# Loads of w_out in quarters, the first tile's u on two queues, and another order in the first two quads

## The chip, the cores and the metric

The kernel runs on one core of a Trainium2 chip. The metric is the time of one execution on the device in microseconds (us); the value that counts is the median of several runs. The core has engines that each work through their own queue in order: PE (matrix products; its weight loads, PEld, overlap them), DVE (VectorE), ACT (ScalarE), POOL (GpSimd) and SP (SyncE, which only issues transfers). Transfers issued by SP or ACT run on 16 shared DMA engines. An engine that comes to an instruction whose input is not there waits, and everything behind it in its queue waits with it.

## The reference

Attention with normalised queries and keys, followed by a feed-forward block. Shapes: q, k, v (8, 12, 448, 64); w_in (768, 1024); w_out (1024, 768); everything is float32 except the three weights of the feed-forward block, which are float64.

```
q_n, k_n = q / sqrt(mean(q*q) + 1e-6) * g_q,  the same for k with g_k
attn = softmax(q_n @ k_n.T / 8);  x = attn @ v, as (3584, 768)
h  = x @ w_in                        # (3584, 1024)
u  = h * softmax(h)
ln = (u - mean(u)) / sqrt(var(u) + 1e-6) * g_ln
out = ln @ w_out                     # (3584, 768)
```

## The kernel before, in words

`fast_path` is what runs; `general_path` stands behind a test at the end and is not entered with these inputs. `fast_path` has two phases, and the order of every engine's work is written out by hand (`manual_schedule`): `unit(f)` runs one step of PE's work and then whatever had been put off with `later(n, f)` to the n-th unit from there. `follow` hangs such a piece of work on a part of the second phase.

**Attention.** 24 quads m of two pairs of heads (a = 2m, b = 2m + 1), so four heads a quad. For a pair, PE makes the scores of three blocks of keys (`scores`, L763), one block of the remaining keys for both pairs (`scores_last`, L776), the values (L796 and L807) and the sums of the exponentials (`sums`, L826). ACT takes the exponentials (L753) of each block; a score tile occupies one of three buffers of PSUM with tag "t" until then, and the tile of the sums, `sm`, comes from the same three. `inverse` (DVE L834, L835, then four small copies on POOL, L840) reads `sm` and so gives its buffer back; `divide` (L847, L848) writes the result `xo`, which `store_x` (SP, L853) puts into DRAM.

The next quads are prepared alongside. For a pair n: `load` (sixteen transfers per quad on SP, L602, each of 32 rows to 32 partitions), `squares` (ACT L624, one buffer), `row_sums` (DVE L632), `fold_sums` (POOL L642, L643), `rsqrt_seed` (ACT L662, L663), `rsqrt_step` (DVE L669 to L672), `normalise` (POOL L681), `qk_transpose` (DVE L691, which writes qkT) and `gain` (ACT L695, which scales the q half of qkT in place; `scores` and `scores_last` need it). The first two quads, m = 0 and m = 1, have an order of their own. `load_v` issues v (L615) and vl (L619) for the next quad.

**Weights.** w_in and w_out come as float64, viewed as pairs of 32-bit words, and are rounded to float32 on the chip, in 28 pieces: 12 of w_in (128 rows by 512 columns) and 16 of w_out (128 rows by 384 columns, 3072 bytes of each row). `load_w` issues the transfer of a piece (SP, L501); `convert_w` turns it into weights with two ACT instructions (L518, L519), two on DVE (L524, L525) and, for w_out, one more on ACT (L530). Twenty pieces are loaded and converted during attention, one a quad, from the fourth quad on (`load_next`, `begin`, `step`); of these the last eight are w_out's, loaded in the quads m = 13 to 20. There are two buffers for raw pieces. The last eight pieces of w_out are loaded together at the start of the second phase, into buffers that the attention's memory becomes, and are converted behind the first parts of the feed-forward block. POOL forms sums and differences of the weights (`combine`, L545).

Partition p = 32 g + j of w_out's piece c must hold row 256 g + 32 c + j, because DVE's transposition of u works in blocks of 32. Before the change one transfer reads all 128 rows through the view `(g c j) n -> c g j n`.

**Feed-forward.** 28 tiles t of 128 tokens in 14 groups g of two. Each product of two matrices is made with seven block products instead of eight (`products`, L918): per group seven with w_in (`in_parts`) and seven with w_out (`out_parts`, two groups later; LAG = 2). A product goes into one of five PSUM banks in turn, "tttoo"; the first is copied by ACT (L929), the others are added up by DVE (L925), and that frees the bank. When a tile's h is complete, its `ff_max` (DVE L972), `ff_exp` (ACT L978), `ff_mult` (DVE L982), `ff_moments` (DVE L990 to L995 and POOL L996), `ff_norm` (DVE L1000) and `ff_spread` follow, each one or more units later. Of each group the second tile comes first. `ff_spread` transposes u in blocks of 32 (DVE L1010) and moves the blocks to their places with sixteen transfers (L1016): a is the block of 32 tokens, g the group of 32 partitions. They are issued by SP, except for the tiles t = 0 and t = 26 (NT - 2), where ACT issues all sixteen. `block_sums` (POOL L898 to L902) makes the sums of blocks that the products need: `xsum` from x, `us` from u. x comes back from DRAM with `load_x` (L871; from the third group on issued by ACT). `load_again` and `check_w` (L554, L560, L561) read the weights once more for a check of their size.

Of the kernel before, what the change touches and what calls it, by code (L numbers as in the profile page):

```python
# [366 lines left out]
def fast_path(  # L367
# [24 lines left out]
    nc = tc.nc  # L392
    B, H, S, D = q.shape
    DM, DFF = moe_w_in.shape
    P = 128
# [5 lines left out]
    KF = DFF // P  # L401
    HO = DM // 2
    NT = B * S // P
# [81 lines left out]
    def load_w(step):  # L485
        src, c, i = step
        n = HO if src is moe_w_out else DFF // 2
        if second is None:
            raw = work.tile([P, DFF // 2, 2], U32, tag="raw", name="raw", bufs=2)[:, 0:n]
        else:  # L490

            tag, size, bufs = ("uT", KF * P, 2 * LAG + 2) if len(raws) % 2 else ("us", 3 * HF * P, 2)
            if tag == "us" and len(raws) >= len(wq) - 4:
                tag, size, bufs = "again", 2 * S, 2
            raw = second.tile([P, size // 2, 2], U32, tag=tag, name="raw", bufs=bufs)[:, 0:n]
        w = src.bitcast(U32)[:, 2 * i * n : 2 * (i + 1) * n]
        if src is moe_w_in:
            w = w[c * P : (c + 1) * P]
        else:
            w = w.rearrange("(g c j) n -> c g j n", g=4, j=32)[c]  # L500
        nc.sync.dma_start(raw.rearrange("p n t -> p (n t)"), w)  # L501
        return raw

    def convert_w(step, raw):
# [116 lines left out]
    def squares(n):  # L621
        d = st[n]
        d["sq"] = work.tile([P, 2 * NB, 32], FP32, tag="sq", name="sq", bufs=1)
        nc.scalar.activation(d["sq"], d["qk"].rearrange("p s b d -> p (s b) d"), AF.Square)  # L624
# [3 lines left out]
    def row_sums(n):  # L628
        m, i = divmod(n, 2)
        if i == 0:  # L630
            norms[m] = {"part": small.tile([P, 2, 2 * NB], FP32, tag="part", name="part", bufs=2)}
        nc.vector.tensor_reduce(norms[m]["part"][:, i], st[n]["sq"], AX, OP.add)  # L632
# [55 lines left out]
    def qk_transpose(n):  # L688
        d = st[n]
        d["qkT"] = work.tile([P, 2, S], FP32, tag="qkT", name="qkT", bufs=3)  # L690
        nc.vector.transpose(d["qkT"].rearrange("p s t -> p (s t)"), d["qkn"].rearrange("p b d -> p (b d)"))  # L691

    def gain(n):
        d = st[n]
        nc.scalar.activation(d["qkT"][:, 0], d["qkT"][:, 0], AF.Copy, scale=gcol[:, KF : KF + 1])  # L695
# [132 lines left out]
    def inverse(m):  # L828


        d = quads[m]
        r = work.tile([P, NB, 32], FP32, tag="r", name="r", bufs=1)
        rc = d["rc"] = small.tile([P, 2, NB], FP32, tag="rc", name="rc")
        nc.vector.transpose(r.rearrange("p b i -> p (b i)"), d["sm"])  # L834
        nc.vector.reciprocal(rc, r[:, :, 0].rearrange("p b -> p () b").to_broadcast([P, 2, NB]))  # L835
        for h in range(2):
            for i in range(2):
                a = 64 * h + 32 * i
                o = 64 * h + 32 * (1 - i)
                nc.gpsimd.tensor_copy(rc[o : o + 32, i], rc[a : a + 32, i])  # L840
# [166 lines left out]
    def ff_spread(t):  # L1007
        d = mt[t]
        ub = second.tile([P, DFF], FP32, tag="ub", name="ub", bufs=2)
        nc.vector.transpose(ub, d["u"])  # L1010
        uT = d["uT"] = second.tile([P, KF, P], FP32, tag="uT", name="uT", bufs=2 * LAG + 2)
        queue = nc.scalar if t in (0, NT - 2) else nc.sync
        for a in range(4):
            x = slice(a * 32, a * 32 + 32)
            for g in range(4):
                queue.dma_start(  # L1016
                    uT[g * 32 : g * 32 + 32, :, x], ub[x].rearrange("j (g c i) -> j g c i", g=4, i=32)[:, g]
                )
# [53 lines left out]
    def unit(f):  # L1072
        nonlocal now
        f()
        now += 1
        due = [x for x in todo if x[0] <= now]
        todo[:] = [x for x in todo if x[0] > now]
        for _, g in sorted(due, key=lambda x: x[0]):
            g()
# [34 lines left out]
    with tc.manual_schedule():  # L1114
# [19 lines left out]
        for m in range(NQ):  # L1134
            a, b = 2 * m, 2 * m + 1

            def outputs():
                values_last(m)
                values(a)


            next1 = m + 1 < NQ
            next2 = m + 2 < NQ
            next3 = m + 3 < NQ
            if m == 0:
# [12 lines left out]
                rsqrt_seed(norms["one", 2])  # L1158
                rsqrt_step(norms["one", 2])
                normalise(2)  # L1160
                add(a)
                unit(lambda: scores(b, 0))
                unit(lambda: scores(b, 1))
                unit(lambda: scores(b, 2))
                squares(3)
                row_sums(3)
                qk_transpose(2)
                fold_one(3)
                gain(2)
                rsqrt_seed(norms["one", 3])  # L1170
                add(b)
                rsqrt_step(norms["one", 3])
                normalise(3)
                load_v(1)
                load(6)
                load(7)
                for _ in range(2):
                    load_next()
                unit(outputs)
                squares(4)  # L1180
                row_sums(4)
                qk_transpose(3)
                unit(lambda: values(b))
                gain(3)
                squares(5)
                unit(lambda: sums(m))
                inverse(m)
                row_sums(5)
                fold_sums(2)
                later(1, lambda m=m: divide(m))  # L1190
                continue
            early = 1 < m and next1
            if early:
                rsqrt_seed(norms[m + 1])
                rsqrt_step(norms[m + 1])
                normalise(a + 2)
                normalise(b + 2)
            if next1:
                load_v(m + 1)
            unit(lambda: scores(a, 0))  # L1200
            store_x(m - 1)
            if early:
                qk_transpose(a + 2)
                if next3:
                    load(a + 6)
            unit(lambda: scores(a, 1))
            unit(lambda: scores(a, 2))
            unit(lambda: scores_last(m))
            add(a)
            unit(lambda: scores(b, 0))  # L1210
            if m == 1:
                rsqrt_seed(norms[m + 1])
                rsqrt_step(norms[m + 1])
                normalise(a + 2)
                normalise(b + 2)
                load(a + 6)
                load(b + 6)
            unit(lambda: scores(b, 1))
            if early:
                qk_transpose(b + 2)  # L1220
                if next3:
                    load(b + 6)
            if m >= NQ // 2:
                combine(w_in, m - NQ // 2)
            unit(lambda: scores(b, 2))
            if m == 1:
                qk_transpose(a + 2)
            if next2:
                squares(a + 4)
                row_sums(a + 4)  # L1230
            if next1:
                gain(a + 2)
            add(b)
            if m == 1:
                qk_transpose(b + 2)
            if next1:
                gain(b + 2)
            if next2:
                squares(b + 4)
                row_sums(b + 4)  # L1240
                fold_sums(m + 2)
            unit(outputs)
            step(m - 2)
            begin(m)
            step(m - 1)
            if m - 1 in sets:
                load_next()
            unit(lambda: values(b))
            if m == NQ - 1:
                block_sums(0, "A", 0)  # L1250
                block_sums(0, "A", 1)
                load_x(1)
            unit(lambda: sums(m))
# [13 lines left out]
        raw = {}  # L1267
# [92 lines left out]
```

## Time and profile before

| | |
|---|---|
| median of 3 runs | 908.34 us (908.28 to 909.74) |
| the profiled execution | 914.59 us |
| its span, first to last instruction | 912.8 us |
| granted PE clock, mean | 0.972 |
| busy: PE, DVE, POOL, ACT | 856.0, 649.6, 320.0, 315.3 us |

A line of the profile names the line of the kernel, the engine, the operation and the tiles, out<-in. In a timeline a line begins with the start and the duration in us, equal neighbours are put together (x8 is eight of them), and the bracket at the end is the idle time of the engine before it and what ended that. "PE L776" is a run on PE, "SPq" or "ACTq" an instruction of that engine's queue such as the issue of a transfer, "DMA raw<-in_moe_w_out_dram" in the chain of waits the time until that transfer had landed. In a table of waits the numbers are the total in us, how many times, and the longest. DMA share is the mean busy share of the 16 DMA engines.

### The profile page before, as it was taken

Reading aid. Unit: us, or ns where it says so; the run is one execution under the profiler, and the core shown is the slowest. Engines: PE = TensorE matmul, PEld = TensorE weight load, DVE = VectorE, ACT = ScalarE, POOL = GpSimd, SP = SyncE. Lnnn points to the kernel's source line nnn. Section 1 sums busy time; section 2 is a strip of 40 time slices with the busy share of each in tenths; the row PEclk is TensorE's granted clock in tenths of the full one; section 3 lists DMA queues with packets and bytes.
Section 4 is the critical chain, followed back from the end, with each engine's and each line's share of the span. In section 5 each row is a group of like instructions: output and inputs, shape, how many; then the busy total and the mean of one; then the engine's idle time right before and its main releaser. Section 6 shows DMA issues by size and latency. Waiting matters only on the chain.

```text
span 912.8 us, 12536 instructions
## 1 busy us (share of the span) xinstructions
PE 856.0 (94%) x4080; PEld 385.4 (42%) x4080; DVE 649.6 (71%) x1028; ACT 315.3 (35%) x475; POOL 320.0 (35%) x434
## 2 busy tenths in 40 slices
PE   5899999999988989968599999999999999999997
PEld 3233333333323323423255454554554554545554
DVE  5778988899868775457876685776866867756642
ACT  5577887787667664150201011011010110110100
POOL 1343444456434453505522421422314214212130
PEclk9999999999989989979799999999999999999999
DMA  6767787886656653232353544445444543331141
GB/s 124 177 148 151 190 191 148 187 192 125 149 128 124 159 133 92 80 114 50 87 148 88 128 115 111 112 85 140 119 90 107 141 101 77 74 64 52 29 110 44
DMA packets 350425, 106.92 MB, mean 117 GB/s; under 512 B 308880, under 2 KB 339600, under 8 KB 350352
## 3 DMA queue, kind: packets, MB, share of 16 engines
q1 hardware_dynamic: 327248, 94.93, 45.4%
q10 hardware_dynamic: 23104, 11.11, 4.6%
q8 instruction: 34, 0.56, 0.3%
q14 instruction: 39, 0.32, 0.1%
HBM read 69.28 MB, written 22.02 MB: 100 GB/s over the span
## 4 chain that ended last, share of the span: by engine, by line
PE 67%; DMA 11%; SPq 8%; DVE 6%; ACT 3%; issue 2%; POOL 2%; ACTq 1%; POOLq 0%; DVEq 0%
PE b L918 49%; PE s L763 6%; PE o L807 6%; DMA raw<-in_moe_w_out_dram 5%; SPq L602 5%; DMA v<-in_v_dram 4%; PE sm L826 3%; SPq L501 2%; ACT E L753 1%; PE s L776 1%; DVE es L786 1%; PE o L796 1%; DMA qk<-in_q_dram 1%; DVE part L632 1%; DMA raw<-in_moe_w_in_dram 1%
## 5 line engine op out<-in xcount | busy, mean ns | idle before, releaser
L918 PE MATMUL b<-w_in,xg 128*128 128x512 f32 x336 | 155.6, 607 | 9.1 <-ACT q L929 5.4
L918 PE MATMUL b<-w_out,uT 128*128 128x384 f32 x448 | 151.4, 486 | 0.0
L753 ACT ACTIVATE E<-s 128x896 f32<-128x896 f32 x168 | 140.2, 931 | 18.5 <-PE s L763 17.3
L763 PE MATMUL s<-qkT 64*64 64x448 f32 x1152 | 129.0, 577 | 3.7 <-DVE r L834 2.1
L918 PE MATMUL b<-w_in,xsum 128*128 128x512 f32 x252 | 119.3, 610 | 7.8 <-DVE h L925 5.3
L918 PE MATMUL b<-w_out,us 128*128 128x384 f32 x336 | 117.9, 495 | 6.1 <-POOL us L899 6.1
L807 PE MATMUL o<-E,v 128*64 128x448 f32 x576 | 113.5, 543 | 0.0
L996 POOL TENSOR_TENSOR he<-he,mhalf 128x1 f32<-128x1 f32 x28 | 17.2, 614 | 269.8 <-DVE he L995 269.8
L918 PEld LDWEIGHTS b<-w_out,uT 128*128 128x128 f32 x448 | 85.2, 190 | 62.0 <-issue 3.4
L918 PEld LDWEIGHTS b<-w_in,xg 128*128 128x128 f32 x336 | 65.1, 195 | 92.3 <-issue 75.1
L929 ACT COPY q<-b 128x512 f32<-128x512 f32 (+1 forms) x28 | 14.9, 530 | 255.2 <-PE b L918 239.7
L978 ACT ACTIVATE u<-h,hmax 128x1024 f32<-128x1024 f32 x28 | 32.2, 1149 | 194.9 <-DVE hmax L972 171.5
L681 POOL TENSOR_TENSOR qkn<-qk,ny 128x896 f32<-128x896 f32 x46 | 77.9, 1714 | 38.9 <-DVE ny L672 21.4
L918 PEld LDWEIGHTS b<-w_out,us 128*128 128x128 f32 x336 | 64.8, 193 | 52.0 <-POOL us L899 6.7
L763 PEld LDWEIGHTS s<-qkT 64*64 64x64 f32 x1152 | 48.4, 168 | 79.9 <-issue 37.8
L918 PEld LDWEIGHTS b<-w_in,xsum 128*128 128x128 f32 x252 | 48.8, 194 | 70.6 <-issue 59.9
L642 POOL COPY ss<-part 32x56 f32<-32x56 f32 x88 | 32.9, 373 | 117.2 <-DVE part L632 114.5
L807 PEld LDWEIGHTS o<-E,v 128*64 128x64 f32 x576 | 39.2, 137 | 72.6 <-issue 65.2
L786 DVE TENSOR_TENSOR es<-E 128x896 f32<-128x896 f32 x48 | 63.9, 1332 | 0.0
L925 DVE TENSOR_TENSOR h<-b,u 128x512 f32<-128x512 f32 x42 | 28.9, 687 | 41.8 <-PE b L918 41.8
L632 DVE TENSOR_REDUCE part<-sq 128x28 f32<-128x896 f32 x46 | 49.5, 1076 | 7.2 <-ACT sq L624 6.5
L925 DVE TENSOR_TENSOR u<-b,u 128x512 f32<-128x512 f32 (+1 forms) x56 | 34.6, 618 | 26.1 <-PE b L918 24.6
(103 smaller groups left out, 999.0 us busy)
## 6 DMA issues: line engine op xcount, KB each, us to landing
uT<-ub SPq DMA_DIRECT2D x416, 32.0 KB
xd<-xo SPq DMA_DIRECT2D x24, 448.0 KB
out_dram<-y SPq DMA_DIRECT2D x27, 384.0 KB
qk<-in_q_dram SPq DMA_DIRECT2D x184, 56.0 KB
qk<-in_k_dram SPq DMA_DIRECT2D x184, 56.0 KB
v<-in_v_dram SPq DMA_DIRECT2D x24, 384.0 KB
raw<-in_moe_w_in_dram SPq DMA_DIRECT2D x12, 512.0 KB
raw<-in_moe_w_out_dram SPq DMA_DIRECT2D x16, 384.0 KB
```

Source lines behind the costliest of these rows:

```text
L602: nc.sync.dma_start(d["qk"][g * 32 : g * 32 + 32, s], src[b, h0 + g // 2].rearrange("(b t) (x d) -> x t b d", t=32, x=2)[g % 2],)
L632: nc.vector.tensor_reduce(norms[m]["part"][:, i], st[n]["sq"], AX, OP.add)
L642: e.tensor_copy(ss[g * 32 : g * 32 + 32], part[o * 32 : o * 32 + 32])
L681: e.tensor_tensor(d["qkn"], d["qk"].rearrange("p s b d -> p (s b) d"), y.rearrange("p b -> p b ()").to_broadcast([P, 2 * NB, 32]), OP.mult,)
L753: nc.scalar.activation(d["E", kc], s[:, :, 0:S], AF.Exp)
L763: nc.tensor.matmul(s[c : c + D, h, 0:S], d["qkT"][hh, 1, keys], d["qkT"][hh, 0, :], start=True, stop=True,)
L786: nc.vector.tensor_tensor(d["es"], d["E", 0], d["E", 1], OP.add)
L807: nc.tensor.matmul(d["o"][h * D : (h + 1) * D, :], quads[n // 2]["v"][:, n % 2 * 2 + h, kc], d["E", kc][:, h], start=False, stop=(kc == NJ ...
L826: nc.tensor.matmul(sm[g : g + 32, :], w, e[:, h], start=(x == 0), stop=(x == len(terms) - 1))
L918: nc.tensor.matmul(o, a[:, c], w[:, i, c], start=(c == 0), stop=(c == last))
L925: nc.vector.tensor_tensor(out, k["o"], k[x], OP.add)
L978: nc.scalar.activation(d["u"], d["h"], AF.Exp, bias=d["nmax"], accum_out=d["s"])
```

## The change

In `load_w`, a piece of w_in is loaded as before, with one transfer. A piece of w_out is loaded with four transfers, one for each group g: 32 whole rows of the source to 32 partitions. In `ff_spread`, the tiles t = 0 and t = 26 have the eight transfers of the blocks a = 0 and 1 issued by SP and those of a = 2 and 3 by ACT. In the quad m = 0, the transposition of pair 3 goes behind `inverse`, and its `gain` moves into the quad m = 1, behind the second block of scores. In the quad m = 1, `gain` of pair b + 2 goes behind `squares` of pair b + 4.

```diff
-        if src is moe_w_in:
-            w = w[c * P : (c + 1) * P]
+            nc.sync.dma_start(to, w[c * P : (c + 1) * P])
         else:
-            w = w.rearrange("(g c j) n -> c g j n", g=4, j=32)[c]
-        nc.sync.dma_start(raw.rearrange("p n t -> p (n t)"), w)
+            for g in range(4):
+                r = (g * KF + c) * 32
+                nc.sync.dma_start(to[g * 32 : g * 32 + 32], w[r : r + 32])
...
-        queue = nc.scalar if t in (0, NT - 2) else nc.sync
         for a in range(4):
+            queue = nc.scalar if a > 1 and t in (0, NT - 2) else nc.sync
...
                 row_sums(4)
-                qk_transpose(3)
                 unit(lambda: values(b))
-                gain(3)
                 squares(5)
                 unit(lambda: sums(m))
                 inverse(m)
+                qk_transpose(3)
                 row_sums(5)
...
             unit(lambda: scores(a, 1))
+            if m == 1:
+                gain(b)
             unit(lambda: scores(a, 2))
...
-            if next1:
+            if next1 and m > 1:
                 gain(b + 2)
             if next2:
                 squares(b + 4)
+            if m == 1:
+                gain(b + 2)
+            if next2:
                 row_sums(b + 4)
```

More of the change, by code (lines that the diff above doesn't have):

```diff
@@ L496, in load_w @@
         w = src.bitcast(U32)[:, 2 * i * n : 2 * (i + 1) * n]
+        to = raw.rearrange("p n t -> p (n t)")
         if src is moe_w_in:
-            w = w[c * P : (c + 1) * P]
+            nc.sync.dma_start(to, w[c * P : (c + 1) * P])
         else:
-            w = w.rearrange("(g c j) n -> c g j n", g=4, j=32)[c]
-        nc.sync.dma_start(raw.rearrange("p n t -> p (n t)"), w)
+            for g in range(4):
+                r = (g * KF + c) * 32
+                nc.sync.dma_start(to[g * 32 : g * 32 + 32], w[r : r + 32])
         return raw
```

## The prediction

> **What bounds the kernel now.** I read the page first, then the busy times by stretch, then the PE timeline, and after that the queue of each engine at the places where PE waits. On the page, the shares of the chain that ended last, by line:
>
> ```profile
> PE 67%; DMA 11%; SPq 8%; DVE 6%; ACT 3%; issue 2%; POOL 2%; ACTq 1%; POOLq 0%; DVEq 0%
> PE b L918 49%; PE s L763 6%; PE o L807 6%; DMA raw<-in_moe_w_out_dram 5%; SPq L602 5%; DMA v<-in_v_dram 4%; PE sm L826 3%; SPq L501 2%; ACT E L753 1%; PE s L776 1%; DVE es L786 1%; PE o L796 1%; DMA qk<-in_q_dram 1%; DVE part L632 1%; DMA raw<-in_moe_w_in_dram 1%
> ```
>
> Two thirds are matmuls, which the change doesn't touch. The rest is w_out pieces (L501 and their landing), the q/k and v loads queued beside them, and small waits. The busy times by stretch say where (columns: stretch, its length, busy time and instructions of PE, PEld, DVE, ACT and POOL, granted clock, DMA share, GB/s):
>
> ```profile
> 0.00:52.00 52.00, 37.95 (x281) 15.12 (x281) 33.66 (x73) 29.29 (x46) 14.07 (x37) 0.97 0.70 144
> 52.00:211.00 159.00, 158.72 (x1340) 58.10 (x1333) 139.17 (x213) 125.41 (x180) 73.99 (x135) 1.00 0.77 173
> 211.00:354.00 143.00, 129.78 (x1016) 44.38 (x1016) 109.26 (x157) 94.30 (x137) 62.33 (x104) 0.94 0.59 133
> 354.00:455.00 101.00, 78.00 (x227) 31.76 (x220) 64.00 (x95) 25.29 (x43) 42.82 (x44) 0.89 0.30 86
> 455.00:912.80 457.80, 451.52 (x1241) 236.08 (x1240) 303.52 (x494) 41.04 (x73) 126.77 (x118) 0.99 0.40 97
> ```
>
> PE is full from 52 to 211 us and again from 455 on, so nothing is to be had there. It stands idle for 14 us before 52, 13 us in 211 to 354, and 23 us in 354 to 455, and in the last two the clock falls to 0.94 and 0.89. These are the stretches in which w_out comes in; w_in, larger by a third, came in during 52 to 211 and cost nothing. In the PE timeline each quad of heads has one run of L776:
>
> ```profile
> 64.17 0.93 PE L776 MATMUL s<-qkT 64*64 64x448 f32 x8
> ...
> 210.96 0.97 PE L776 MATMUL s<-qkT 64*64 64x448 f32 x8
> ...
> 353.91 0.93 PE L776 MATMUL s<-qkT 64*64 64x448 f32 x8
> ```
>
> Eleven quads took 146.79 us, 13.34 each; the next nine took 142.95, 15.88 each: 22.9 us more than nine at 13.34.
>
> **Part 1, the w_out pieces.** Who waits for them, in the table of waits; how long one takes to land, in the chain by time; and how busy the 16 DMA engines are while almost nothing but w_out is moving:
>
> ```profile
> ACT tmp L518 <- DMA raw<-in_moe_w_out_dram: 52.1, 16, 6.4
> ```
> ```profile
> 244.99 8.21 DMA raw<-in_moe_w_out_dram
> ```
> ```profile
> 376.00:403.00 27.00, 19.52 (x41) 7.92 (x39) 12.08 (x19) 9.01 (x16) 6.74 (x7) 0.91 0.26 103
> ```
>
> A share of 0.26 with eight transfers queued is 4 engines of 16 at full load: 384 KB run at 103 GB/s, some 3.8 us a piece, and whatever is queued behind them on these four engines waits too. The old source view begins with the 4 groups g, the new ones with 32 rows, like the q/k loads. So I read the change as: 4 engines before, 16 after. The Trainium skill ("DMA: Bandwidth & Descriptors", section "Why a DMA increments its semaphore by 16 and not by 1") says that such a DMA uses the largest number of engines up to 16 that divides the slowest dimension of both sides: 4 before, 16 after; the 0.26 agrees with the first half, and by this rule the sum is the one below.
>
> The attention quads. SP's queue:
>
> ```profile
> 206.35 1.98 SPq L602 DMA_DIRECT2D qk<-in_q_dram  x4
> 208.37 3.33 SPq L602 DMA_DIRECT2D qk<-in_k_dram  x4
> 211.81 0.61 SPq L501 DMA_DIRECT2D raw<-in_moe_w_out_dram  x1
> ...
> 215.02 5.32 SPq L602 DMA_DIRECT2D qk<-in_q_dram  x4
> ...
> 228.04 0.58 SPq L501 DMA_DIRECT2D raw<-in_moe_w_out_dram  x1
> ```
>
> Four q/k issues cost 1.98 us, or 0.50 each; right behind a w_out piece, v and xo they cost 5.32, since the four engines are still full. SP comes round in 16.23 us (211.81 to 228.04), later than PE needs it, so loads come late and ACT, whose queue is in order, holds back the exponentials behind L518. With 16 engines the jam goes, and the piece lands before ACT asks. What is late next is SP itself: w_out, v, vl and xd take 3.21 us (211.81 to 215.02), eight q/k issues 5.46 with one long one among them (206.35 to 211.81), the other eight about 4.1 (twice 1.98 and the gaps): 12.8. Three more issues at 0.50 make 14.3, against 13.34 for a quad, so SP falls behind by up to 0.96 in each of the eight quads that load a piece, 7.7 in all. Queued behind those issues are v, the xo store and the next q/k; they are asked for a quad ahead, which takes up some. Between 0 and 7.7 I take the middle, 3.7. Gain: 22.9 - 3.7 = 19.2 (15.2 to 22.9).
>
> The last eight pieces come when the attention's buffers are freed. SP, then DVE, whose converts L524/L525 stand between the additions that free PE's banks:
>
> ```profile
> 372.52 19.55 SPq L501 DMA_DIRECT2D raw<-in_moe_w_out_dram  x8
> 420.06 10.81 SPq L1016 DMA_DIRECT2D uT<-ub  x16
> ```
> ```profile
> 380.88 1.24 DVE L524 SCALAR_TENSOR_TENSOR tmp<-raw,tmp 128x384 uint32<-128x384 uint32 x1 [4.66 <-ACT tmp L519]
> ...
> 409.69 0.68 DVE L925 TENSOR_TENSOR u<-b,q 128x512 f32<-128x512 f32 x1
> ```
> ```profile
> 380.88:409.69 28.81, 20.60 (x38) 8.01 (x37) 16.59 (x24) 13.41 (x25) 2.02 (x2) 0.82 0.32 116
> ```
>
> From the first convert to the first addition after the last one DVE works 16.59 of 28.81 us; the rest it waits for pieces. Afterwards 32 issues at 0.50 take 16 us from 372.5, a piece about every 2 us instead of 3.8, the last landing near 391. The first convert moves up by 2.8 to 378.1 (of the 8.4 us from its piece's issue, 372.52, to 380.88, the 3.8 of transfer become 1.0); then DVE's own 16.6 us is the bound, plus some 1.9 for waits that remain among ACT, DVE and the pieces: 378.1 + 16.6 + 1.9 = 396.6 instead of 409.69. Gain 13.1 (9 if SP needs 0.6 an issue and DVE waits twice as long; 15 if DVE never waits).
>
> **Part 2, the first tile's u.** ACT's queue:
>
> ```profile
> 423.88 10.68 ACTq L1016 DMA_DIRECT2D uT<-ub  x16
> 434.61 1.15 ACT L978 ACTIVATE u<-h,hmax 128x1024 f32<-128x1024 f32 x1 [23.39 <-DMA uT<-ub]
> ```
>
> Sixteen issues hold ACT for 10.7 us, and the next tile's exponential, then DVE's product and PE's next copy, come after them. Eight issues fewer: 5.4 us earlier; the order behind is unchanged and DVE and POOL follow at once, so I count 5.4 (2 if DVE's other work fills in). The eight go to SP behind the other tile's sixteen (420.06 + 10.81 + 8 × 0.68 = 436.3); behind them wait the loads for the check, which nobody needs soon.
>
> The last tile but one is split as well. Tail of SP, POOL and PE:
>
> ```profile
> 871.69 10.68 SPq L1016 DMA_DIRECT2D uT<-ub  x16
> ```
> ```profile
> 883.85 1.26 POOL L898 TENSOR_TENSOR us<-uT 128x512 f32<-128x512 f32 x1 [12.86 <-DMA uT<-ub]
> ```
> ```profile
> 888.97 2.82 PE L918 MATMUL b<-w_out,uT 128*128 128x384 f32 x8
> ```
>
> Sixteen issues end at 882.4 and have landed by 883.85, 1.5 later. With eight more SP ends at 887.7 and they land at 889.2, 0.2 after PE wants this tile (888.97). I charge 0.2 (0 to 1).
>
> **Part 3, order in the first two quads.** DVE and PE:
>
> ```profile
> 30.20 1.11 DVE L691 STREAM_TRANSPOSE qkT<-qkn 128x896 f32<-128x896 f32 x1 [0.81 <-POOL qkn L681]
> 31.23 0.61 DVE L834 STREAM_TRANSPOSE r<-sm 128x448 f32<-128x448 f32 x1
> ...
> 46.53 1.09 DVE L632 TENSOR_REDUCE part<-sq 128x28 f32<-128x896 f32 x1 [1.58 <-ACT sq L624]
> ```
> ```profile
> 31.89 1.01 PE L763 MATMUL s<-qkT 64*64 64x448 f32 x8 [1.63 <-DVE r L834]
> ...
> 50.67 0.98 PE L776 MATMUL s<-qkT 64*64 64x448 f32 x8 [1.42 <-ACT E L753]
> ```
>
> The transpose of the fourth pair waits for POOL, and the inverse behind it frees the bank that PE wants. Put first, the inverse starts at 29.4 (30.20 less the 0.81 of waiting): 1.8 earlier. The scaling moved behind the first exponentials lets ACT start them earlier, but the pair's scores then wait for it; both fit into the same 1.8. In the second quad squares go ahead of the scaling that waits for DVE's transpose, so L632 loses its 1.58 wait. Only single DVE, ACT and four small POOL instructions move, no DMA. Gain 1.8 + 1.6 = 3.4 (1 to 4.5).
>
> **Sum.** 3.4 + 19.2 + 13.1 + 5.4 - 0.2 = 40.9. The profiled execution took 914.59 us (span 912.8), 6 us over the median of 908.34; none of the terms depends on that, so I take them from both: 873.7 there, and 867.4 for the median. Best ends: 4.5 + 22.9 + 15 + 5.4 = 47.8, 860.5. Weak ends: 1 + 15.2 + 9 + 2 - 1 = 26.2, 882.
>
> **The rivals.** *SP becomes the bound:* its 14.3 is taken up by nothing, and an issue costs 0.6 rather than 0.50. Quads 14.6 instead of 13.34: 8 × 1.26 = 10 lost instead of 3.7, and some 3 more in the last eight pieces: 877. For: SP has hardly a gap from 206 on. Against: loads are asked for a quad ahead. *DVE or ACT keeps the old pace after 372:* 5 of the 13.1 come: 875.5. For: DVE is busy 64 of 101 us there, and closing the gaps leaves it nearly full. *The pieces land no sooner* (memory, not four engines, sets 103 GB/s), but SP hides its issues: only parts 2 and 3 stay, 8.6: 900. Against: w_in's stretch moved 173 GB/s. *Slower:* the pieces land no sooner and each of 48 more issues lies on the path: 48 × 0.50 = 24 against 8.6 gained: 924. It decides once a split saves a piece's waiting by less than (24 - 8.6)/16 = 1.0 us; ACT's wait alone is now 52.1/16 = 3.3 a piece. The Trainium skill ("DMA: Bandwidth & Descriptors", section "Rules for kernel authors") speaks for this one: transfers to disjoint parts of the partitions serialize on the same engines, so one over 128 partitions should be used; no transfer quoted above tests it for 32 rows of 3 KB.
>
> **How the numbers follow.** Forecast 0.58 (861 to 872), SP bound 0.20, DVE or ACT 0.12, no sooner 0.04, slower 0.03, better than all ends 0.03. Range 860 to 882 leaves out the last three. Measurement of this kernel tells 0.2% (1.8 us) from no change. Faster by more: 0.96; within: 0.01; slower: 0.03.
>
> **What the profile after would show.** The DMA share well above 0.26 while the last eight pieces come, ACT's wait for raw near zero of 52.1, quads at 13.3 to 14.3 between the L776 runs, ACT's next exponential some 5 us after its first uT issue, and PE's wait for us L899 at 454 come some 37 us earlier. I am wrong if ACT still waits microseconds for raw, if the q/k issues behind a piece still take 5 us for four, or if DVE has gaps of several us between converts.

## The result, and the profile after

| | before | after |
|---|---|---|
| median | 909.04 us (908.28 to 912.4) | 870.77 us (870.16 to 872.16) |
| ratio, 95% interval | 1 | 0.9574 (0.9547 to 0.9602) |
| span of the profiled execution | 912.8 us | 868.3 us |
| granted PE clock, mean | 0.972 | 0.993 |

The change takes 38.3 us off the median; 40.9 were predicted. In the lines of after, numbers from the second half of the kernel are 2 to 4 higher: L501 is now L504, L518 L521, L602 L605, L776 L779, L899 L902, L918 L921, L925 L928, L978 L981, L1016 L1020; the kernels of the experiments have numbers of their own. On the page, the chain that ended last:

```profile
PE 77%; SPq 7%; DMA 4%; POOL 3%; issue 3%; DVE 3%; ACT 1%; ACTq 0%; POOLq 0%; DVEq 0%
PE b L921 51%; PE o L810 9%; PE s L766 9%; PE sm L829 5%; SPq L605 4%; DMA qk<-in_k_dram 2%; SPq L504 2%; PE s L779 2%; PE o L799 1%; DMA v<-in_v_dram 1%; ACT E L756 1%; POOL w_out L548 1%; SPq L1020 0%; DVE part L635 0%; POOL ss L645 0%
```

PE's share went from 67 to 77%, DMA's from 11 to 4%, and the landing of w_out pieces, 5% before, is no longer listed. The busy times by stretch, with the columns of before (the last stretch is shorter because the kernel ends sooner):

```profile
0.00:52.00 52.00, 40.92 (x311) 17.00 (x313) 36.90 (x77) 33.21 (x51) 16.45 (x38) 1.00 0.69 142
52.00:211.00 159.00, 158.56 (x1336) 57.67 (x1336) 138.64 (x213) 125.23 (x179) 74.74 (x134) 1.00 0.78 175
211.00:354.00 143.00, 142.17 (x1100) 51.52 (x1093) 119.62 (x170) 98.06 (x143) 74.08 (x119) 1.00 0.63 150
354.00:455.00 101.00, 89.69 (x221) 42.91 (x220) 84.56 (x126) 23.77 (x43) 41.46 (x39) 0.95 0.46 112
455.00:868.20 413.20, 406.94 (x1124) 212.76 (x1122) 273.65 (x446) 35.40 (x62) 114.27 (x106) 1.00 0.39 94
```

PE's idle time from 211 to 354 us went from 13.2 us to 0.8, and the clock there from 0.94 to 1.00. From 354 to 455 PE still stands idle for 11.3 of 101 us, with the clock at 0.95; of that more below. The waits for w_out pieces in ACT's queue (total, times, longest), and the PE timeline at the same three quads as before (and at the end of the longest of the last nine, which began at 274.63):

```profile
ACT tmp L521 <- DMA raw<-in_moe_w_out_dram: 4.2, 3, 2.8
```
```profile
60.29 0.56 PE L779 MATMUL s<-qkT 64*64 64x448 f32 x4
...
207.67 0.98 PE L779 MATMUL s<-qkT 64*64 64x448 f32 x8
...
289.02 0.98 PE L779 MATMUL s<-qkT 64*64 64x448 f32 x8 [0.83 <-ACT E L756]
...
329.16 0.93 PE L779 MATMUL s<-qkT 64*64 64x448 f32 x8
```

52.1 us of waiting became 4.2, the longest single wait 2.8. The nine quads with loads took 121.49 us (329.16 - 207.67), 13.50 each, where they had taken 142.95. SP's queue shows why, and that SP is still no faster than PE:

```profile
209.60 1.81 SPq L504 DMA_DIRECT2D raw<-in_moe_w_out_dram  x4
...
213.94 2.34 SPq L605 DMA_DIRECT2D qk<-in_q_dram  x4
...
222.64 2.77 SPq L504 DMA_DIRECT2D raw<-in_moe_w_out_dram  x4
...
236.60 2.22 SPq L504 DMA_DIRECT2D raw<-in_moe_w_out_dram  x4
...
307.31 1.80 SPq L504 DMA_DIRECT2D raw<-in_moe_w_out_dram  x4
```

The four issues of a piece take 1.81 us, 0.45 each. The four q/k issues that come after a piece, v and xo take 2.34 us where they took 5.32: SP no longer stands behind full engines. A round of SP takes 13.04 and then 13.96 us (from 209.60 to 222.64 and to 236.60), against 16.23 before. But over all seven rounds, from 209.60 to 307.31, it is 13.96 on average, longer than a quad of 13.34: SP falls 4.3 us behind PE. PE lost 1.4 us in the nine quads (121.49 against nine at 13.34), 1.05 of it in the one that ends at 289.02, 14.39 us long. In it ACT waits for a piece, and later PE for an exponential (0.83):

```profile
283.37 0.95 ACT L627 ACTIVATE sq<-qk 128x896 f32<-128x896 f32 x1 [1.56 <-DMA raw<-in_moe_w_out_dram]
```

The last eight pieces and what follows, in three stretches: from the last L779 to the first product with w_in, from there to the first addition after the last convert, and from there to the first product with us. First before, then after:

```profile
353.91:364.96 11.05, 11.05 (x92) 3.77 (x84) 5.83 (x7) 5.07 (x7) 6.78 (x5) 1.00 0.40 113
364.96:409.69 44.73, 36.52 (x78) 15.15 (x75) 23.06 (x33) 15.17 (x28) 12.68 (x16) 0.89 0.27 99
409.69:454.56 44.87, 30.08 (x62) 12.49 (x60) 34.79 (x55) 4.70 (x9) 23.01 (x23) 0.87 0.31 67
```
```profile
329.16:340.21 11.05, 11.05 (x92) 3.76 (x84) 5.83 (x7) 5.07 (x7) 6.78 (x5) 1.00 0.40 113
340.21:371.07 30.86, 30.86 (x76) 13.79 (x73) 24.33 (x34) 16.20 (x29) 13.75 (x16) 1.00 0.47 143
371.07:409.32 38.25, 26.94 (x64) 11.26 (x62) 34.70 (x55) 3.80 (x7) 23.02 (x23) 0.95 0.36 78
```

The second stretch is 13.87 us shorter, and PE is now busy through all of it at the full clock. While SP issues the last eight pieces in 32 transfers, the DMA share is 0.67, where it was 0.26:

```profile
348.14:362.86 14.72, 14.72 (x36) 6.56 (x35) 12.73 (x16) 8.99 (x17) 8.10 (x7) 1.00 0.67 199
```

The third stretch is 6.62 us shorter, and DVE is busy for 34.70 of its 38.25 us. In it, ACT's queue and then PE:

```profile
385.27 5.36 ACTq L1020 DMA_DIRECT2D uT<-ub  x8
390.67 1.15 ACT L981 ACTIVATE u<-h,hmax 128x1024 f32<-128x1024 f32 x1 [18.87 <-DMA uT<-ub]
```
```profile
399.37 2.82 PE L921 MATMUL b<-w_out,uT 128*128 128x384 f32 x8 [1.16 <-DMA uT<-ub]
409.32 2.93 PE L921 MATMUL b<-w_out,us 128*128 128x384 f32 x4 [7.13 <-POOL us L902]
...
844.55 2.85 PE L921 MATMUL b<-w_out,uT 128*128 128x384 f32 x8 [0.20 <-DMA uT<-ub]
```

Eight issues hold ACT for 5.36 us instead of 10.68, as predicted, and the exponential follows 5.40 us after the first of them. PE still waits 7.13 us for the sums of u at 409 us, the longest wait that is left. The first product with us begins 45.24 us sooner than before (454.56); the prediction's terms up to there add up to 41.1, and its list of signs has 37. At the end, the tile t = 26 lands 0.20 us too late: the 0.2 that was charged.

### The profile page after: what moved, and what is told of

The parts are those of the page before. It is cut to its first block, busy times and chain, and to the rows that moved or that the text cites. A ratio compares the mean times of both kernels' runs of the same rounds, so it can differ in the third digit from the quotient of the medians.

```text
span 868.3 us, 12637 instructions
## 1 busy us (share of the span) xinstructions
PE 838.3 (97%) x4080; PEld 381.9 (44%) x4080; DVE 653.4 (75%) x1028; ACT 315.7 (36%) x475; POOL 321.0 (37%) x434
## 4 chain that ended last, share of the span: by engine, by line
PE 77%; SPq 7%; DMA 4%; POOL 3%; issue 3%; DVE 3%; ACT 1%; ACTq 0%; POOLq 0%; DVEq 0%
PE b L921 51%; PE o L810 9%; PE s L766 9%; PE sm L829 5%; SPq L605 4%; DMA qk<-in_k_dram 2%; SPq L504 2%; PE s L779 2%; PE o L799 1%; DMA v<-in_v_dram 1%; ACT E L756 1%; POOL w_out L548 1%; SPq L1020 0%; DVE part L635 0%; POOL ss L645 0%
## 5 line engine op out<-in xcount | busy, mean ns | idle before, releaser
L921 PE MATMUL b<-w_out,uT 128*128 128x384 f32 x448 | 152.0, 488 | 1.4 <-DMA uT<-ub 1.4
L921 PE MATMUL b<-w_in,xg 128*128 128x512 f32 x336 | 151.3, 593 | 0.6 <-DVE h L928 0.6
L921 PE MATMUL b<-w_out,us 128*128 128x384 f32 x336 | 118.0, 495 | 7.1 <-POOL us L902 7.1
L766 PE MATMUL s<-qkT 64*64 64x448 f32 x1152 | 123.3, 555 | 1.1 <-DVE qkT L749 0.8
L921 PE MATMUL b<-w_in,xsum 128*128 128x512 f32 x252 | 115.1, 592 | 2.4 <-POOL xsum L902 2.4
L921 PEld LDWEIGHTS b<-w_out,uT 128*128 128x128 f32 x448 | 85.4, 191 | 64.1 <-issue 3.2
L981 ACT ACTIVATE u<-h,hmax 128x1024 f32<-128x1024 f32 x28 | 32.2, 1149 | 190.9 <-DVE hmax L975 172.0
L921 PEld LDWEIGHTS b<-w_in,xg 128*128 128x128 f32 x336 | 63.6, 190 | 79.4 <-issue 73.7
L921 PEld LDWEIGHTS b<-w_out,us 128*128 128x128 f32 x336 | 64.8, 193 | 53.0 <-POOL us L902 7.7
L921 PEld LDWEIGHTS b<-w_in,xsum 128*128 128x128 f32 x252 | 47.8, 190 | 63.1 <-issue 59.3
L928 DVE TENSOR_TENSOR h<-b,u 128x512 f32<-128x512 f32 x42 | 28.9, 688 | 41.8 <-PE b L921 41.8
L928 DVE TENSOR_TENSOR u<-b,u 128x512 f32<-128x512 f32 (+1 forms) x56 | 34.6, 619 | 26.1 <-PE b L921 24.5
```

The source lines that it names most:

```text
L766: nc.tensor.matmul(s[c : c + D, h, 0:S], d["qkT"][hh, 1, keys], d["qkT"][hh, 0, :], start=True, stop=True,)
L921: nc.tensor.matmul(o, a[:, c], w[:, i, c], start=(c == 0), stop=(c == last))
L928: nc.vector.tensor_tensor(out, k["o"], k[x], OP.add)
L981: nc.scalar.activation(d["u"], d["h"], AF.Exp, bias=d["nmax"], accum_out=d["s"])
```

## The experiments

My theory: the w_out pieces cost what they did because one transfer with an outer dimension of 4 kept to 4 of the 16 DMA engines; that is worth about 32 us, the first tile's u about 5, the order about 3. The rivals: that smaller transfers or more of them in flight help, whatever their shape; that SP's issues are the bound; and that what the order of the first quads gains doesn't reach the end.

**The parts alone.** Four kernels on one chip beside the kernel before (910.07 us).

Part 1 alone: the four transfers of 32 rows, and nothing else of the change.

```diff
...
-            w = w.rearrange("(g c j) n -> c g j n", g=4, j=32)[c]
-        nc.sync.dma_start(raw.rearrange("p n t -> p (n t)"), w)
+            for g in range(4):
+                r = (g * KF + c) * 32
+                nc.sync.dma_start(to[g * 32 : g * 32 + 32], w[r : r + 32])
```

> Only the four transfers per piece of w_out; the two queues for u and the order of the first quads as before. Theory A (the piece ran on 4 of 16 DMA engines, and that is what held up the quads and the last eight pieces): from the quad m = 14 to m = 23 the traces went from 142.95 to 121.49 us and the first convert to the addition after the last one moved 13.9 us, 35 in all; medians moved by 38.3, of which the other two parts should be 8 to 9, so this one is worth 30 to 35 us: 874 to 879 us. The first L776 of m = 2 stays at 50.7 us. Rival B (the parts are not independent: the jam in SP's queue also needs the earlier start of the first quads, or ACT's sixteen issues eat what the pieces give back): less than 24 us, above 884.

Measured: 876.87 us, ratio 0.9636 (0.962 to 0.9652). In the table of waits ACT's wait for raw is down, and in the PE timeline the nine quads take 120.15 us:

```profile
ACT tmp L521 <- DMA raw<-in_moe_w_out_dram: 5.5, 4, 2.8
```
```profile
210.61 0.97 PE L779 MATMUL s<-qkT 64*64 64x448 f32 x8
...
330.76 0.93 PE L779 MATMUL s<-qkT 64*64 64x448 f32 x8
```

By the ratio part 1 is worth 33.1 us (31.7 to 34.6) of 910.07, nearly the whole gain. The prediction had 32.3 for its two terms.

Part 2 alone: the u of the first tile and of the last but one on two queues.

```diff
-        queue = nc.scalar if t in (0, NT - 2) else nc.sync
         for a in range(4):
+            queue = nc.scalar if a > 1 and t in (0, NT - 2) else nc.sync
```

> Only the split of the first and the last but one u tile over SP and ACT. Theory A: ACT is free 5.3 us earlier, and all that follows (the exponential, DVE's product, PE's copy, us) moves with it: 5 us less, minus 0.2 to 0.7 at the end: 903.5 to 904.5 us, PE's wait for us ends 5.3 us earlier counted from the first convert. Rival B: us waits for POOL's own order or for u on SP, which now has 24 transfers to issue; then the exponential comes earlier but us does not: within 1.5 us of before.

Measured: 903.61 us, ratio 0.9937 (0.9917 to 0.9957), so 5.7 us (3.9 to 7.6).

Part 3 alone: the order of the first two quads.

```diff
-                qk_transpose(3)
                 unit(lambda: values(b))
-                gain(3)
...
                 inverse(m)
+                qk_transpose(3)
...
             unit(lambda: scores(a, 1))
+            if m == 1:
+                gain(b)
...
-            if next1:
+            if next1 and m > 1:
                 gain(b + 2)
             if next2:
                 squares(b + 4)
+            if m == 1:
+                gain(b + 2)
+            if next2:
                 row_sums(b + 4)
```

> Only the order of inverse, transposition and scaling in the first two quads. Theory A: the 3.9 us by which the L776 of m = 2 comes earlier (50.67 to 46.79) stay to the end: 904.5 us. Rival B: in the quads that load w_out the pace is set by SP and the transfers, not by PE, so an earlier start is waited away there: L776 of m = 2 at 46.8 as well, but the L776 of m = 23 less than 1.5 us earlier, and the time above 907.

Measured: 908.69 us, ratio 0.9989 (0.9973 to 1.0006): 1.0 us (-0.5 to 2.5), not to be told from nothing. The PE timeline of this kernel at the third and the fourth quad:

```profile
46.84 0.98 PE L776 MATMUL s<-qkT 64*64 64x448 f32 x8 [0.67 <-ACT E L753]
...
62.10 0.61 PE L776 MATMUL s<-qkT 64*64 64x448 f32 x4 [0.84 <-ACT E L753]
```

The third quad begins at 46.84 instead of 50.67, 3.8 us sooner. One quad on, 62.10 against 64.17, it is 2.1: PE waits 0.84 us more for an exponential there, and the rest of the loss isn't assigned. The rival was nearer in the time, but its mechanism is not what the trace shows: the run of the last quad begins at 344.49, 5.75 us sooner than in the trace of the unchanged kernel below, where it should have come less than 1.5 sooner. This profiled execution, 904.03 us, was the fastest of twelve; what the typical one loses, and where, stays open.

The kernel before once more, unchanged, to see how much two executions of one kernel differ.

> The kernel before, unchanged, profiled once more: its profiled execution took 914.59 us and its median is 908.3 to 909.0, while the traces of before and after differ by 44.5 us and the medians by 38.3. Theory A: the 6 us are waits that vary from one execution to the next, in the quads that load w_out (142.95 us from m = 14 to m = 23 in the first trace): a profile of 908 to 910 us has 137 us there and the same stretches elsewhere. Rival B: profiling adds them everywhere: again 914 to 915 us, with 143 there.

Measured: 909.64 us, ratio 1.0002. Its profiled span is 907.8 us, 5.0 less than that of the first profile, and the PE timeline shows most of that in one place:

```profile
210.79 0.96 PE L776 MATMUL s<-qkT 64*64 64x448 f32 x8
...
350.24 0.93 PE L776 MATMUL s<-qkT 64*64 64x448 f32 x8
```

The nine quads took 139.45 us here, 142.95 in the first profile, and 136.61 and 135.36 in those of parts 2 and 3, which have the old loads too. So what the slow loads cost is not a fixed number: 3.5 us apart in two executions of one kernel, 7.6 over these four traces of three kernels. In seven traces with the quarters, these nine quads took 120.15 to 122.89 us.

**What about the four transfers helps.** First one transfer, but of 128 consecutive rows:

```diff
-        if src is moe_w_in:
-            nc.sync.dma_start(to, w[c * P : (c + 1) * P])
-        else:
-
-            for g in range(4):
-                r = (g * KF + c) * 32
-                nc.sync.dma_start(to[g * 32 : g * 32 + 32], w[r : r + 32])
+        nc.sync.dma_start(to, w[c * P : (c + 1) * P])
```

> The changed kernel with each piece of w_out loaded by one transfer of 128 consecutive rows, as w_in's pieces are, in place of four transfers of 32 rows; the product with w_out then uses rows of w_out in another order, so this run is only for its time. Theory A (what the four transfers gain is the spread over all 16 DMA engines): one transfer whose outer dimension is 128 rows does the same with a quarter of the issues. ScalarE's wait for raw pieces stays at a few us, the nine quads with loads take 120 to 121.5 us as with the quarters, the queue's issues no longer come near its bound, and the kernel takes 866 to 871 us. Rival B (it is the size or the number of the transfers that counts, a single large one being slow whatever its shape): the waits for raw are back and the kernel takes 895 to 910 us.

Measured: 869.72 us, ratio 0.9552 (0.9526 to 0.9578), the same as the change. SP's queue has 8 issues in place of 32 for the last eight pieces. In the busy times, the DMA share while they land is 0.97, and from the first convert to the first addition after the last PE has no gap:

```profile
348.93 3.70 SPq L498 DMA_DIRECT2D raw<-in_moe_w_out_dram  x8
```
```profile
350.00:357.50 7.50, 7.50 (x19) 3.37 (x18) 6.81 (x8) 5.04 (x9) 5.30 (x5) 1.00 0.97 342
353.26:371.88 18.62, 18.62 (x44) 8.18 (x44) 18.34 (x25) 14.50 (x26) 6.95 (x6) 1.00 0.45 152
```

So neither the number nor the size of the transfers made the gain: one large one does it if its outer dimension is long. A quarter of the issues brings nothing further that can be told from noise. SP's round falls to 13.28 us with it (seven rounds from 210.18 to 303.16), PE's pace, but the nine quads take 120.75 us, no less than the 120.80 that they take on average in seven traces with quarters: the few us by which SP falls behind with four don't show. Then the other way, two transfers of 64 rows:

```diff
-            for g in range(4):
-                r = (g * KF + c) * 32
-                nc.sync.dma_start(to[g * 32 : g * 32 + 32], w[r : r + 32])
+            v4 = w.rearrange("(g c j) n -> c g j n", g=4, j=32)[c]
+            for h in range(2):
+                nc.sync.dma_start(to[h * 64 : h * 64 + 64], v4[2 * h : 2 * h + 2])
```

> The changed kernel with each piece in two transfers of 64 rows, each with an outer dimension of 2 and runs of 32 rows behind it. Theory A (the number of engines of a transfer follows its outer dimension): each transfer uses 2 engines, a piece needs about twice the time that it needed as one transfer of outer dimension 4, the DMA share in the stretch of the last eight pieces is about 0.13, eight pieces take about 60 us there, and the kernel is slower than before the change: 940 to 980 us. Rival B (smaller transfers, more of them in flight, are what helps): between the 870 of the change and the 908 of before, about 885 us.

Measured: 961.23 us, ratio 1.057 (1.0538 to 1.0602): 52 us slower than before, with transfers half as large and two in place of one. The table of waits, SP's queue and the busy times while the last eight pieces come and nothing else is moving:

```profile
ACT tmp L520 <- DMA raw<-in_moe_w_out_dram: 106.8, 16, 10.1
```
```profile
392.64 48.91 SPq L503 DMA_DIRECT2D raw<-in_moe_w_out_dram  x16
```
```profile
410.00:449.00 39.00, 11.56 (x17) 4.38 (x18) 9.11 (x15) 7.81 (x14) 0.00 (x0) 0.65 0.13 52
```

ACT's wait doubled, and an issue took SP 3.06 us (48.91/16) against 0.46 in the change; I read that as SP waiting for room, which no view shows by itself. 52 GB/s and a share of 0.13, two engines' worth, stand against 103 and 0.26 with one transfer of outer dimension 4: half, as expected. This kills the rival of smaller transfers. It also speaks against slower engines or a slower memory as the cause: among the trace's DMA packets, those of 3072 bytes, the rows of w_out, took 0.123 us each in the kernel before and 0.124 here, but before, four of them were in flight at a time (23.8 of the 27 us from 376 to 403), and here two (42.4 of the 45 us from 410 to 455). So transfers that wait behind one another used no more engines than one alone. The Trainium skill ("DMA: Bandwidth & Descriptors", section "Why a DMA increments its semaphore by 16 and not by 1") has the number of engines follow the slowest dimension: for 128, 32, 4 and 2 the order of the times agrees, its 4 agrees with the share of 0.26 before, and its 2 with the 0.13 here.

Eight transfers of 16 rows:

```diff
             for g in range(4):
-                r = (g * KF + c) * 32
-                nc.sync.dma_start(to[g * 32 : g * 32 + 32], w[r : r + 32])
+                for h in range(2):
+                    r = (g * KF + c) * 32 + h * 16
+                    p = g * 32 + h * 16
+                    nc.sync.dma_start(to[p : p + 16], w[r : r + 16])
```

> The changed kernel with each piece in eight transfers of 16 rows: the same bytes over the same engines with 32 more issues in every eight pieces. Theory A (SyncE's issue of transfers is near its bound already with four per piece): at 0.45 us for an issue a quad grows by 1.8 us of issue, of which 1.3 to 1.8 shows, 10 to 16 us over nine quads; the last eight pieces are 64 issues, 29 us against 14.7, which adds 8 to 14 us; 888 to 900 us in all. Rival B (the issues lie beside other work and have room): less than 875 us.

Measured: 898.54 us, ratio 0.9878 (0.9848 to 0.9908). SP's queue in the quads and at the last eight pieces:

```profile
225.25 3.65 SPq L505 DMA_DIRECT2D raw<-in_moe_w_out_dram  x8
...
240.39 4.55 SPq L505 DMA_DIRECT2D raw<-in_moe_w_out_dram  x8
...
320.56 4.64 SPq L505 DMA_DIRECT2D raw<-in_moe_w_out_dram  x8
```
```profile
363.15 30.59 SPq L505 DMA_DIRECT2D raw<-in_moe_w_out_dram  x64
```

A round of SP takes 15.14 us from 225.25 to 240.39 and 15.89 on average over the six rounds to 320.56. PE's nine quads take 135.25 us: the first three still 13.26 to 13.50 us each, the other six 15.05 to 16.37. From the fourth on SP sets the pace. The 64 issues at 0.48 us take 30.59 us, and the stretch from the first product with w_in to the addition after the last convert is 45.10 us, 14.2 longer than with four transfers. With four transfers SP is the slower engine too, by 0.6 us a round; over eight pieces that doesn't reach PE, presumably because the loads are asked for a quad ahead. With eight it is slower by 2.5, and that shows.

**What is left at 409 us.** PE's 7.13 us wait there is for `us` on POOL. In the trace after, POOL makes the four sums over x first (402.27 to 406.66 us), though the sums over u are wanted sooner. Three things put otherwise:

```diff
-            queue = nc.scalar if a > 1 and t in (0, NT - 2) else nc.sync
+            queue = nc.scalar if t == NT - 2 or (t == 0 and a > 1) or (t == 1 and a == 3) else nc.sync
...
-            follow(p, 2 if g > LAG else 4, lambda: block_sums(g - LAG, "U", 0))
+            follow(p, 2 if g > LAG else 1, lambda: block_sums(g - LAG, "U", 0))
```

> The changed kernel with three things put otherwise: the transfers of the second-last tile's u all on ScalarE's queue as before the change; one more transfer of the second tile's u on ScalarE's queue; and the sums over the first u blocks follow one part earlier, so that they stand ahead of the other sums on GpSimd. Theory A (TensorE's 7.13 us wait for the sums of u, and the late second-last tile, are the loss that is left of the change): the wait shrinks to 1 to 3 us and 0.2 us come back at the end: 864 to 868 us. Rival B (VectorE, dense from 371 to 414 us, is the bound of that stretch, and whatever GpSimd does earlier only moves the wait): 869.5 to 872 us.

Measured: 867.27 us, ratio 0.9526 (0.9498 to 0.9554), 4.4 us below the change by the two ratios, whose intervals touch. In the PE timeline the wait fell from 7.13 to 0.78 us, and a new one came:

```profile
404.08 2.82 PE L921 MATMUL b<-w_out,us 128*128 128x384 f32 x8 [0.78 <-POOL he L999]
...
433.85 2.93 PE L921 MATMUL b<-w_in,xsum 128*128 128x512 f32 x3 [2.58 <-DVE y L928]
```

Behind it, in the timelines of SP and DVE, stands the second reading of the weights:

```profile
407.71 19.91 SPq L1020 DMA_DIRECT2D uT<-ub  x28
427.71 1.02 SPq L557 DMA_DIRECT2D again<-in_moe_w_in_dram  x2
```
```profile
432.19 0.62 DVE L563 TENSOR_REDUCE extent<-again 128x1 f32<-128x448 f32 x1 [6.31 <-DMA again<-in_moe_w_in_dram]
```

The transfer is issued only at 427.71, behind 28 issues of u, and DVE, which takes its work in order, stands 6.31 us before the reduction that needs it; the addition that PE wants is behind that. The last four kernels were run beside each other on one chip. The change itself:

> The changed kernel itself, beside the three others on one chip, so that they can be compared with it and not only with the kernel before. 869 to 872 us.

Measured: 871.82 us, ratio 0.9592 (0.9571 to 0.9613). The change without part 3, that is with the diff of part 3 taken back (its removed lines stand again, its added ones don't):

> The changed kernel with the order of the first quads put back to that of before; the quarters and the first tile's u on two queues stay. Theory A (the 3.9 us that the order gains before the third quad are partly taken back in that quad: 1.8 us are left at its end in five of the six traces that have the order): 871 to 873 us, 1 to 2 above the changed kernel of this call. Rival B (the whole gain stays, as in the changed kernel's own trace): 873.5 to 875 us. Rival C (nothing stays): the same as the changed kernel within 0.5 us.

Measured: 871.52 us, ratio 0.9577 (0.9556 to 0.9598), 0.3 below the change: rival C, nothing stays. The profiled executions of the two differ by 2.5 us the other way (spans 869.8 and 867.3), so a single profile of each would have said that the order gains.

The kernel with the three things put otherwise, the early sums over u among them, and in addition the second reading fourteen parts of PE's work later (the products of one group; its third transfer is issued at 454.07 us instead of 425.72):

```diff
-            follow(parts, (2 * LAG + 1 + 2 * (x // 3)) * 7 - 7 * LAG + (0, 4, 5)[x % 3], lambda x=x: check_next(x))
+            follow(parts, (2 * LAG + 1 + 2 * (x // 3)) * 7 + (0, 4, 5)[x % 3], lambda x=x: check_next(x))
```

> The changed kernel with the second-last tile's u all on ScalarE's queue again, a fourth part of the second tile's u on ScalarE's queue, the first sums over u ahead of the other sums on GpSimd, and the second reading of the weights for their extent two groups later, so that it doesn't stand in SyncE's queue behind the first tiles' u. Theory A (without the late reading the 6.5 us gained before the product with us are kept: the 2.58 us wait of TensorE at 434 us and the half clock behind it are gone): 863 to 866 us. Rival B (another wait of the same size takes its place on VectorE or SyncE, or the end of the kernel now waits for the check): 867 us or more.

Measured: 862.55 us (861.93 to 863.62), ratio 0.9482 (0.9462 to 0.9502): 9.3 us below the change on the same chip, somewhat better than the theory's best. The 2.58 us wait is gone. The busy times of 405.3 to 415.5 us, in the change and here, show that the 7.13 us wait had cost more than itself:

```profile
405.30:415.50 10.20, 6.18 (x10) 3.46 (x11) 9.08 (x12) 2.85 (x5) 6.35 (x6) 0.50 0.57 125
```
```profile
405.30:415.50 10.20, 9.29 (x29) 5.23 (x30) 10.13 (x12) 2.85 (x5) 6.54 (x6) 1.00 0.39 91
```

In the change the granted clock falls to 0.50 during the wait, at 405.3 us, and stays there until 415.5, 6.2 us after PE has work again. How long it stays isn't fixed: in the second trace of the change, behind a wait of 7.15 us, it is back at 412.0, 2.8 us after PE has work. In the kernel with the late reading, where the wait is 0.74 us, it is 1.00 throughout, and PE gets 29 products done in these 10.2 us instead of 10.

The same without part 3:

> The kernel with the early sums over u and the late second reading, and with the order of the first quads put back to that of before. Theory A (the order is worth 1 to 2 us): that much above the kernel with it in this call. Rival B (worth nothing): within 0.5 us of it.

Measured: 863.66 us (863.29 to 864.67), ratio 0.9498 (0.9477 to 0.9518), 1.1 above the kernel with it: theory A at its low end, though the intervals of the two ratios overlap.

## Why the prediction was right

Its steps, with what the traces showed. The second column is before against after, one trace each; the third is the difference of the means over all traces with and without that part (for the quads and the last eight, old loads in four traces and quarters in seven; for the order six without and eight with it; for the last two rows four without and seven with the split).

| step | predicted | two traces | all traces |
|---|---|---|---|
| order of the first quads (up to the quad at 211 us) | 3.4 | 3.3 | 2.1 |
| nine attention quads with w_out | 19.2 | 21.5 | 17.8 |
| last eight pieces | 13.1 | 13.9 | 13.8 |
| first tile's u | 5.4 | 6.6 | 5.9 |
| after the product with us | -0.2 | -0.7 | -0.1 |

**Four engines before, sixteen after.** Right, and shown: four packets in flight before, two with an outer dimension of 2 (share 0.13), and a share of 0.97 with one transfer of 128 rows, which takes the same time as four of 32. With four of 32 rows the share stays at 0.67, while SP issues them in 14.72 us. The rivals "no sooner" and "slower" fell with it. The Trainium skill's rule ("DMA: Bandwidth & Descriptors", section "Rules for kernel authors") against transfers to disjoint parts of the partitions, which I had set beside the slower case, holds here in this much: four transfers to 32 partitions each are no faster than one with 128 rows outermost (870.77 and 869.72 us). But the transfer that was replaced wasn't that one, and against it splitting gains 33 us.

**SP falls behind by 3.7.** The term was too large, and the step that had it wrong is how much of SP's lag reaches PE. SP's round was 13.96 us on average, up to 14.68, near the 14.3; with 13.34 for a quad it fell 4.3 us behind in seven rounds. (The piece's issues took more than I had counted, 1.80 to 3.03 us for four; a round's sixteen q/k issues less, 8.70 with the gaps between them, 213.94 to 222.64, where I had 5.46 and 4.1.) I let half of the largest lag through. The nine quads lost 1.4 us against nine at 13.34 in this trace, and 0.1 to 2.8 in the seven traces with quarters, 0.7 on average, the same as with one transfer a piece (120.75): nearly all of a lag of this size doesn't reach PE. That the loads are asked for a quad ahead explains it, but no run had them asked for later. The rival "SP becomes the bound" named the right engine, but it takes eight transfers a piece to get there.

**The last eight.** DVE's timeline of after has the first convert and the addition after the last one:

```profile
352.94 0.76 DVE L527 SCALAR_TENSOR_TENSOR tmp<-raw,tmp 128x384 uint32<-128x384 uint32 x1 [1.10 <-ACT tmp L522]
```
```profile
371.07 0.68 DVE L928 TENSOR_TENSOR u<-b,q 128x512 f32<-128x512 f32 x1
```

The first convert came 3.19 us sooner after the first product with w_in (15.92 us before, 12.73 after), where I had 2.8, and 18.13 us later came the addition, where I had 18.5. I took DVE for the bound. PE is just as full there, 30.86 of 30.86 us, so a faster DVE alone might have won nothing more; that wasn't tried. The rival in which DVE or ACT keeps the old pace is refuted by that stretch.

**First tile's u.** Right in mechanism: ACT's sixteen issues became eight, 5.3 us. The rest of the measured 5.9 comes and goes with other waits in that stretch, which without the split took 43.57 to 44.87 us in four traces and with it 38.25 to 38.42 in seven.

**The order.** This is the term that failed in size. I read the waits of 1.8 and 1.6 us correctly: the third quad does begin 3.9 us sooner in the two traces. But I took a start 3.4 us earlier for an end 3.4 us earlier. Part of it is gone a quad later (why is only in part known), and in the medians it is worth 1.0 alone (-0.5 to 2.5), -0.3 in the change and 1.1 in the last kernel.

**The median.** I wrote that none of the terms depends on the profiled execution's 6 us over the median. That was wrong: in another execution of the same kernel 3.5 of 5.0 us were in the nine quads, the stretch from which the largest term was read. The two traces differ by 44.5 us, the medians by 38.3. With the 139.45 us of the second trace the quads' excess over 120.06 would have been 19.4 instead of 22.9, and the term 15.7 rather than 19.2. The errors went both ways: the quads' excess and the order were taken too large, SP's 3.7 was mostly not lost. That the sum came out within 3.4 us is in part luck. One reading beside the sum was wrong as well: w_in is not larger than w_out by a third, only its pieces are (12 of 512 KB against 16 of 384).

## What to carry to other kernels

Read the DMA share of a stretch in which one kind of transfer is alone: 0.26 with eight transfers issued one behind the other is a transfer that uses a quarter of the engines, and its view's outermost dimension is the place to look. Splitting helps only as far as it makes that dimension longer; beyond that each issue costs the queue 0.45 us, and whether this shows depends on how much longer the round of the issuing engine is than the work of one step, and for how many steps (a round of 14.0 against 13.3 us was all but free over eight rounds; one of 15.9 cost 15 us over nine quads). A wait that is closed early in a kernel is worth what is left of it at the end; and where waits vary between executions, take two profiles of the same kernel before a term is sized from one.

## What the runs showed of the hardware that was not expected

Transfers that wait behind one another didn't spread over the engines that stood idle: with eight of outer dimension 4, four packets were in flight and the share was 0.26; with sixteen of outer dimension 2, two and 0.13. And a long wait of PE costs more than its length: behind the 7.13 us at 409 us PE worked for another 6.2 us at half the clock, 2.8 in a second trace of the same kernel. The kernel in which this wait was 0.74 us had the full clock there.
